# Moving four small packed matmul blocks of a batch: one adjacent pair in the slot, two singles behind the attention-score matmuls

## Chip, cores, metric

One core of one Trainium2 chip. The metric is the device time of one execution in microseconds (us). The experiments ran in three later calls, each with the kernel before beside it; the record names a different chip for each of these calls, so runs of different calls are best compared by their ratios to the kernel before.

## The reference, cut to what matters

```python
# q, k, v: (8, 8, 576, 64); p: (8, 8, 32, 64)
p_packed = sm_attn(p, k, v)             # 32 packed rows per head
out = sm_attn(q, p_packed, p_packed)    # second attention, over 32 rows only
x = out.transpose(0, 2, 1, 3).reshape(4608, 512)
h = x @ w_in                            # 512 -> 2048
y = (h * cos(h)) @ w_out                # 2048 -> 512
```

The kernel does not form `x`. Since `x` is attention weights times `p_packed`, it computes the product `p_packed @ w_in` ("PPW") once per batch, and then `h` as attention weights times PPW.

## The kernel before

It works batch by batch. A *slot* of a batch has 16 steps. Each has one *hidden block* (four matmuls of 288 columns, cosine on ScalarE, product on VectorE) and some *output matmuls* (512 columns, `fill`) of the batch before, which give TensorE other work while a product is pending. Between two slots stand the two kinds of attention scores. The four PPW blocks of the next batch (`ppw(b, 0..3)`) are placed in the slot, two steps apart.

All the matmuls below write to PSUM, the memory in which the pool `A` lies. A block can start only when a PSUM buffer is free, which is when the last instruction that reads it has ended.

```python
A = ctx.enter_context(tc.tile_pool(name="psA", bufs=3, space=PSUM))   # 3 buffers for ALL of these
def psa(dt=FP32):
    return A.tile([128, 2, 512 if dt == FP32 else 1024], dt, name="psA", tag="A")

def ppw(b, n):                      # L175: eight matmuls on 64x32 tiles of the array, side by side
    ...
    ps = psa()
    for x in range(4):
        for y in range(2):
            r = slice(64 * y, 64 * y + 64)
            nc.tensor.matmul(ps[32 * x:32 * x + 32, y, :], ppT[b % 2][r, 2 * x + y, :],
                             w_in_bf[r, x, n * 512:(n + 1) * 512], start=True, stop=True)
    copy((V, ACT)[n % 2], PPW[b][:, :, n * 512:(n + 1) * 512], ps)

def h_mm(b, fc):                    # one hidden block
    ps = psa()
    ...                             # 4 matmuls, 128x128
    ACT.activation(out=csv, in_=ps[:, :, 0:HS], func=AF.Sin, bias=pihalf)
    def rest():
        V.tensor_tensor(out=gT..., in0=ps[:, :, 0:HS], in1=csv, op=ALU.mult)   # frees ps
        ...
    return rest

def slot(s, pieces, hooks):
    left = filler[1]
    for fc in range(NFC):           # 16 steps
        rest = h_mm(s, fc)
        while pieces and pieces[0][0] == fc:
            pieces.pop(0)[1]()
        rest()
        while hooks and hooks[0][0] == fc:
            hooks.pop(0)[1]()
        done = left - filler[1]
        fill((left * (fc + 1)) // NFC - done)

for s in range(2, B):
    ...
    s2(s)                           # second-stage scores: 64x32 tiles, two psa() buffers
    fill(8)
    if nxt:
        s1(s + 1)                   # first-stage scores of the next batch: the same
        ...
    fill(4); sums2(s, 0); fill(5); sums2(s, 1); normalise(s); fill(13)
    pieces = [(1, pw(2, 2)), (4, pw(2, 3))] if s == 2 else []
    if nxt:
        pieces += [(5, lambda: pp(s + 1))] + [(8 + 2 * n, pw(s + 1, n)) for n in range(4)]
    slot(s, pieces, [])
```

Matmuls run in the order of the program, and `psa()` hands out the three buffers in the order in which their last readers stand in the program.

The softmax here doesn't subtract the row's maximum and nothing guards it: scores larger than these inputs give would overflow.

Of the kernel before, what the change touches and what calls it, by code (L numbers as in the profile page):

```python
# [15 lines left out]
def kernel(  # L16
# [37 lines left out]
    V, ACT, G = nc.vector, nc.scalar, nc.gpsimd  # L54

    w_in_bf = const.tile([128, 4, DF], BF16, name="w_in_bf")
    w_out_bf = const.tile([128, NFC, DM], BF16, name="w_out_bf")
# [5 lines left out]
    p_raw = const.tile([128, 2 * B, D], FP32, name="p_raw")  # L63
    p_bf = const.tile([128, 2 * B, 2, D], BF16, name="p_bf")
# [6 lines left out]
    a2u, lns, a2n, PPW = {}, {}, {}, {}  # L71

    def copy(eng, out, in_):
        if eng is ACT:
            ACT.copy(out=out, in_=in_)  # L75
        else:
            eng.tensor_copy(out=out, in_=in_)  # L77

    def psa(dt=FP32):
        return A.tile([128, 2, 512 if dt == FP32 else 1024], dt, name="psA", tag="A")  # L80

    def load(n, b):
        bf[n, b] = bf_pool.tile([TP, H, C * D], BF16, name=n + "bf", tag=n + "bf")
        G.dma_start(out=bf[n, b], in_=srcs[n][b].rearrange("h (p c) d -> p h (c d)", c=C))  # L84
# [6 lines left out]
    def xbar(n, b):  # L91
        t = xT[n, b] = att_pool.tile([128, H * 3, TP], BF16, name=n + "T", tag=n + "T")
        nc.sync.dma_start_transpose(out=t, in_=bf[n, b].rearrange("p h x -> p (h x)"))
# [13 lines left out]
    def pack_p(b0, b1):  # L107
        ng = 2 * (b1 - b0)
        ps = psa(BF16)
        flat = ps.rearrange("p a x -> p (a x)")  # L110
        for g in range(ng):
            nc.tensor.transpose(flat[:, g * 128:(g + 1) * 128],
                                p_bf[:, 2 * b0 + g].rearrange("p t d -> p (t d)"), ident)
        V.tensor_copy(out=P2[:, b0:b1].rearrange("p b h n -> p (b h n)"), in_=flat[:, 0:ng * 128])

    def scores(lhs, rhs):
        ps = []
        for y in range(2):
            t = psa()
            for x in range(4):  # L120
                for e in range(2):
                    r = slice(64 * e, 64 * e + 64)
                    h = 2 * x + y
                    nc.tensor.matmul(t[32 * x:32 * x + 32, e, 0:HS], lhs[r, h, :],  # L124
                                     rhs[r, 3 * h:3 * h + 3, :], start=True, stop=True)
            ps.append(t)
        return ps

    def s1(b):
        ps = scores(P2[:, b], xT["k", b])  # L130
        sm = small.tile([128, 2], FP32, name="sums1")
        for y in range(2):
            ACT.activation(  # L133
                out=a1[b % 2][:, y, :, 0:TP].rearrange("p (e m) x -> p e m x", e=2),
                in_=ps[y][:, :, 0:HS].rearrange("p e (m x) -> p e m x", m=3),
                func=AF.Exp, scale=scale, accum_out=sm[:, y:y + 1])
        sums1[b] = sm
# [20 lines left out]
    def pp(b):  # L158
        ps = psa()
        for hp in range(4):  # L160
            for j in range(C):
                c = 2 * (j % 3) + j // 3
                nc.tensor.matmul(ps[:, 0, hp * 64:(hp + 1) * 64], vp[b][:, c, hp * 128:(hp + 1) * 128],  # L163
                                 a1T[b][0:TP, :, j, 32 * hp:32 * hp + 32], start=(j == 0), stop=(j == C - 1))
        pv = ps[:, 0, 0:256].rearrange("p (a y x) -> p a y x", a=4, y=2)
        t = ppT[b % 2].rearrange("p (a y) x -> p a y x", y=2)
        for y in range(2):
            r = slice(64 * y, 64 * y + 64)
            V.tensor_copy(out=t[r, :, y, :], in_=pv[r, :, y, :])
        for y in range(2):  # L170
            r = slice(64 * y, 64 * y + 64)
            z = slice(64 - 64 * y, 128 - 64 * y)
            ACT.copy(out=t[z, :, y, :], in_=pv[r, :, y, :])  # L173

    def ppw(b, n):  # L175
        if b not in PPW:
            PPW[b] = ppw_pool.tile([128, 2, DF], BF16, name="PPW", tag="PPW")
        ps = psa()
        for x in range(4):
            for y in range(2):  # L180
                r = slice(64 * y, 64 * y + 64)
                nc.tensor.matmul(ps[32 * x:32 * x + 32, y, :], ppT[b % 2][r, 2 * x + y, :],  # L182
                                 w_in_bf[r, x, n * 512:(n + 1) * 512], start=True, stop=True)
        copy((V, ACT)[n % 2], PPW[b][:, :, n * 512:(n + 1) * 512], ps)

    def s2(b):
        a2u[b] = att_pool.tile([128, 2, S], BF16, name="a2u", tag="a2u")
        ps = scores(ppT[b % 2], xT["q", b])
        for y in range(2):
            ACT.activation(out=a2u[b][:, y].rearrange("p (e x) -> p e x", e=2),  # L190
                           in_=ps[y][:, :, 0:HS], func=AF.Exp, scale=rs1[b][:, y:y + 1])
# [91 lines left out]
    def set_filler(b):  # L283
        fill(1000)
        filler[0] = out_gen(b)
        filler[1] = 16 * n_chunks(b)

    def fill(n):
        while n > 0 and filler[1] > 0:
            next(filler[0])  # L290
            filler[1] -= 1
            n -= 1

    def load_w_in(n):
        G.dma_start(out=w_in_bf[:, :, n * 512:(n + 1) * 512],
                    in_=moe_w_in.rearrange("(a p) n -> p a n", p=128)[:, :, n * 512:(n + 1) * 512])

    def load_w_out(n):
        G.dma_start(out=w_out_bf[:, n * 4:(n + 1) * 4, :],
                    in_=moe_w_out.rearrange("(a p) n -> p a n", p=128)[:, n * 4:(n + 1) * 4, :])  # L300

    def dup_p(a, b):
        for t in range(2):
            V.tensor_copy(out=p_bf[:, a:b, t, :], in_=p_raw[:, a:b, :])

    def load_w_in(n):
        G.dma_start(out=w_in_bf[:, :, n * 512:(n + 1) * 512],
                    in_=moe_w_in.rearrange("(a p) n -> p a n", p=128)[:, :, n * 512:(n + 1) * 512])

    def load_w_out(n):  # L310
        G.dma_start(out=w_out_bf[:, n * 4:(n + 1) * 4, :],
                    in_=moe_w_out.rearrange("(a p) n -> p a n", p=128)[:, n * 4:(n + 1) * 4, :])

    def dup_p(a, b):
        for t in range(2):
            V.tensor_copy(out=p_bf[:, a:b, t, :], in_=p_raw[:, a:b, :])

    def warm(n):
        for _ in range(n):
            nc.tensor.matmul(wps, wz[:, 0:128], wz, start=True, stop=True)  # L320
# [41 lines left out]
    pe_T("q", 0, (V, ACT, V))  # L362
    s2(0)
    ppw(0, 0)
    sums2(0, 0)
    sums2(0, 1)
# [42 lines left out]
    def slot(s, pieces, hooks):  # L409
        left = filler[1]  # L410
        for fc in range(NFC):
# [9 lines that stand above are left out]
    def pw(b, n):  # L421
        return lambda: ppw(b, n)

    def begin_loads(b):
        G.tensor_copy(out=gate, in_=xT["k", b][0:1, 0, 0:1])
        for n, i in (("v", b), ("q", b), ("k", b + 1)):
            load(n, i)
# [2 lines left out]
    xbar("q", 2)  # L430
    xbar("k", 3)
    slot(1, [(1, pw(1, 2)), (4, pw(1, 3)), (7, lambda: pp(2)), (9, lambda: pack_p(3, B)),
             (11, pw(2, 0)), (14, pw(2, 1))], [(8, lambda: begin_loads(3))])

    for s in range(2, B):
        nxt = s + 1 < B
        set_filler(s - 1)
        ACT.preload_act_table_set(EXP_SET)  # L438
        if nxt:
            permute_v(s + 1)  # L440
        s2(s)
        fill(8)
        if nxt:
            s1(s + 1)
            xbar("q", s + 1)
            if s + 2 < B:
                xbar("k", s + 2)
            a1_xbar(s + 1)
            recips(s + 1)
            G.tensor_copy(out=gate, in_=a1T[s + 1][0:1, 0, 0, 0:1])  # L450
        fill(4)
        sums2(s, 0)
        fill(5)
        sums2(s, 1)
        normalise(s)
        fill(13)
        for n, b in (("v", s + 2), ("q", s + 2), ("k", s + 3)):
            if b < B:
                load(n, b)
        pieces = [(1, pw(2, 2)), (4, pw(2, 3))] if s == 2 else []  # L460
        if nxt:
            pieces += [(5, lambda: pp(s + 1))] + [(8 + 2 * n, pw(s + 1, n)) for n in range(4)]
        slot(s, pieces, [])
        fill(1000)
    set_filler(B - 1)
# [32 lines left out]
```

## Time and profile before

| | before |
|---|---|
| median | 264.84 us (264.78 to 265.21, 3 runs) |
| TensorE (PE) busy | 244.6 of 263.0 us |
| ScalarE (ACT), VectorE (DVE) busy | 182.7, 158.5 us |

From the page of the kernel before, its first part: busy time, share of the span, number of instructions for each engine.

```profile
PE 244.6 (93%) x2037; PEld 132.1 (50%) x2037; DVE 158.5 (60%) x248; ACT 182.7 (69%) x276; POOL 53.5 (20%) x67
```

TensorE is the limit. What counts is what it does that is not streaming of columns. The next lines are the PE part of the timeline of the kernel before, slot 4 (columns: start, duration, engine, line, operation, operands, number merged). L221 is a hidden block, L271 output matmuls, L182 a PPW block. `128*128` and `64*32` are the sizes of the tiles into which the array is divided: the tiling mode. A PPW block and the scores use 64x32 tiles, the other matmuls shown here the whole array.

```profile
153.59 0.65 PE L221 MATMUL psA<-a2n,PPW 128*128 128x288 bf16 x4
154.17 0.41 PE L182 MATMUL psA<-w_in_bf,ppT 64*32 64x512 bf16 x8
154.51 0.82 PE L271 MATMUL ot<-w_out_bf,gT 128*128 128x512 bf16 x3
155.17 0.65 PE L221 MATMUL psA<-a2n,PPW 128*128 128x288 bf16 x4
155.66 0.81 PE L271 MATMUL ot<-w_out_bf,joint 128*128 128x512 bf16 x3
156.31 0.65 PE L221 MATMUL psA<-a2n,PPW 128*128 128x288 bf16 x4
```

Read starts, not durations: matmuls overlap. The step from 155.17 to 156.31 has no PPW block and takes 1.14 us. The step from 153.59 to 155.17 has one and takes 1.58 us. So a block costs 0.44 us, and 512 columns stream in only about 0.215 us (three 512-column output matmuls, from 155.66 to 156.31, take 0.65). The other 0.23 us is on both sides of the block. The Trainium skill, "TensorEngine Tiling (Array Packing)", Key Properties, states that changing the tiling mode drains the TensorE; this trace agrees in that each change costs time, and it gives the size. Whether all of it is the drain, or a part is the weight loads at the boundary, is open; "mode change" below means the 0.23 us.

The end of slot 4 in the same kernel, with the lines of ScalarE and VectorE that matter. L225 is the cosine, L228 the product, L124 the scores (two kinds), L190 the exponential of the second-stage scores.

```profile
160.62 0.65 PE L221 MATMUL psA<-a2n,PPW 128*128 128x288 bf16 x4
161.31 0.74 ACT L225 ACTIVATE cosT<-psA,pihalf 128x576 bf16<-128x576 f32 x1
162.06 0.44 PE L124 MATMUL psA<-qT,ppT 64*32 64x288 bf16 x16
162.08 0.76 DVE L228 TENSOR_TENSOR gT<-psA,cosT 128x576 bf16<-128x576 f32 x1 [0.82 <-ACT cosT L225]
162.43 1.90 PE L271 MATMUL ot<-w_out_bf,gT 128*128 128x512 bf16 x8
164.26 0.32 PE L124 MATMUL psA<-kT,P 64*32 64x288 bf16 x8
164.86 0.32 PE L124 MATMUL psA<-kT,P 64*32 64x288 bf16 x8 [0.28 <-ACT a2u L190]
```

The last hidden block starts at 160.62, and its buffer is free at 162.84, when the product ends: 2.22 us. The scores pass without a wait, because they take older buffers. The first-stage scores at 164.26 wait half-way for an exponential (the bracket shows the idle time and its cause).

Four lines of the list of waits of PE in the kernel before (columns: total us, times, longest). The wait in the last line lies in the start-up, at 25 us, and is not of a slot:

```profile
PE psA L221 <- DVE gT L228: 3.1, 10, 0.5
PE psA L124 <- ACT a2u L190: 1.1, 3, 0.5
PE psA L221 <- DVE PPW L77: 0.7, 2, 0.5
PE psA L182 <- DVE gT L228: 0.6, 1, 0.6
```

### The profile page before, as it was taken

How to read it: one execution, taken by the hardware profiler on the slowest of the kernel's cores; microseconds unless marked ns; L12 is line 12 of the kernel's file. 1: busy time of each engine (PE TensorE's matmuls, PEld its weight loads, DVE VectorE, ACT ScalarE, POOL GpSimd, SP SyncE). 2: the span in 40 equal slices, each digit the busy share in tenths (PEclk: the TensorE clock that was granted, in tenths of full speed). 3: DMA queues.
4: the chain of work that ended last, by engine and by line, in shares of the span. 5: the costliest groups of instructions: out<-in, count | busy, mean ns of one | idle time of the engine just before them, and what ended most of it. 6: DMA issues, size and time to landing. Idle time of an engine off the chain costs nothing.

```text
span 263.0 us, 5065 instructions
## 1 busy us (share of the span) xinstructions
PE 244.6 (93%) x2037; PEld 132.1 (50%) x2037; DVE 158.5 (60%) x248; ACT 182.7 (69%) x276; POOL 53.5 (20%) x67
## 2 busy tenths in 40 slices
PE   8758779998989999999999999999999999999993
PEld 3433446455534555456445644464446554565452
DVE  2446886748853787358835685378735873578110
ACT  1358882497698757987798768877897678886000
POOL 8523002440422220504050302220040000000000
PEclk9997999999999999999999999999999999999998
DMA  6999999999399899399949992899194111111232
GB/s 95 203 226 206 206 204 197 192 186 201 47 203 203 189 165 187 73 193 173 221 95 184 168 221 75 159 188 176 47 158 113 40 42 40 40 46 36 80 82 80
DMA packets 62919, 37.09 MB, mean 141 GB/s; under 512 B 35520, under 2 KB 58304, under 8 KB 62896
## 3 DMA queue, kind: packets, MB, share of 16 engines
q0 software_dynamic: 23168, 18.81, 47.1%
q1 hardware_dynamic: 39568, 17.83, 31.5%
q8 instruction: 16, 0.26, 0.4%
q10 hardware_dynamic: 160, 0.13, 0.2%
q14 instruction: 7, 0.06, 0.1%
HBM read 37.22 MB, written 9.44 MB: 177 GB/s over the span
## 4 chain that ended last, share of the span: by engine, by line
PE 66%; DMA 13%; ACT 9%; DVE 7%; issue 2%; POOL 1%; DVEq 0%; ACTq 0%; POOLq 0%
PE ot L271 39%; PE psA L221 17%; DMA kbf<-in_k_dram 7%; DMA w_in_bf<-in_moe_w_in_dram 5%; DVE gT L228 4%; ACT cosT L225 3%; PE psA L182 2%; PE psA L163 2%; DVE PPW L77 2%; ACT PPW L75 1%; ACT L438 1%; PE psA L124 1%; PE ot L260 1%; PE psA L198 1%; PE psA L102 1%
## 5 line engine op out<-in xcount | busy, mean ns | idle before, releaser
L271 PE MATMUL ot<-w_out_bf,gT 128*128 128x512 bf16 x512 | 132.1, 380 | 0.0
L225 ACT ACTIVATE cosT<-psA,pihalf 128x576 bf16<-128x576 f32 x128 | 94.0, 742 | 32.0 <-PE psA L221 30.7
L228 DVE TENSOR_TENSOR gT<-psA,cosT 128x576 bf16<-128x576 f32 x128 | 94.9, 754 | 33.7 <-ACT cosT L225 32.6
L221 PE MATMUL psA<-a2n,PPW 128*128 128x288 bf16 x512 | 83.4, 285 | 5.5 <-DVE gT L228 3.1
L221 PEld LDWEIGHTS <-PPW 128*128 128x128 bf16 x512 | 49.9, 97 | 43.0 <-issue 13.0
L271 PEld LDWEIGHTS <-gT 128*128 128x128 bf16 x512 | 47.0, 98 | 42.8 <-issue 7.1
L232 POOL COPY joint<-gT 128x512 bf16<-128x512 bf16 x16 | 9.7, 614 | 111.1 <-DVE gT L228 111.1
L208 DVE SCALAR_TENSOR_TENSOR a2n<-a2u,r,lns 128x576 bf16<-128x576 bf16 x16 | 12.4, 815 | 20.1 <-ACT lns L206 20.1
L77 DVE COPY osb<-ot 128x512 f32<-128x512 f32 (+1 forms) x19 | 12.7, 670 | 15.1 <-PE ot L271 12.0
L75 ACT COPY osb<-ot 128x512 f32<-128x512 f32 (+1 forms) x18 | 10.3, 574 | 15.0 <-PE ot L271 10.1
L77 DVE CAST PPW<-psA 128x1024 bf16<-128x1024 f32 x16 | 19.5, 1220 | 1.5 <-PE psA L182 1.2
L75 ACT CAST PPW<-psA 128x1024 bf16<-128x1024 f32 x16 | 16.1, 1005 | 2.6 <-PE psA L182 2.6
L77 POOL COPY vp<-vbf 96x3072 bf16<-96x3072 bf16 x6 | 16.5, 2749 | 1.2 <-DMA vbf<-in_v_dram 1.2
L182 PE MATMUL psA<-w_in_bf,ppT 64*32 64x512 bf16 x256 | 13.4, 393 | 2.2 <-DMA w_in_bf<-in_moe_w_in_dram 1.5
L271 PE MATMUL ot<-w_out_bf,joint 128*128 128x512 bf16 x48 | 12.9, 380 | 0.0
L190 ACT ACTIVATE a2u<-psA,rs 128x576 bf16<-128x576 f32 x16 | 11.0, 738 | 2.5 <-PE psA L124 2.4
L200 ACT ACTIVATE lns<-psA 128x576 f32<-128x576 f32 x16 | 10.5, 658 | 2.3 <-PE psA L198 2.3
L133 ACT ACTIVATE a<-psA 128x576 bf16<-128x576 f32 x16 | 10.3, 651 | 2.6 <-PE psA L124 2.6
L173 ACT CAST ppT<-psA 64x128 bf16<-64x128 f32 x16 | 4.2, 260 | 10.8 <-PE psA L102 6.5
L142 DVE RECIPROCAL r<-sums 128x2 f32<-128x2 f32 x8 | 1.3, 160 | 16.5 <-ACT a L133 16.5
L84 POOL DMA_DIRECT2D kbf<-in_k_dram x8 | 6.3, 786 | 21.2 <-PE psA L102 17.3
L320 PE MATMUL wps<-wz 128*128 128x512 bf16 x25 | 9.4, 537 | 1.2 <-DVE wz L342 1.2
(55 smaller groups left out, 152.4 us busy)
## 6 DMA issues: line engine op xcount, KB each, us to landing
kbf<-in_k_dram POOLq DMA_DIRECT2D x8, 576.0 KB, 11.4
vbf<-in_v_dram POOLq DMA_DIRECT2D x8, 576.0 KB, 6.8
qbf<-in_q_dram POOLq DMA_DIRECT2D x8, 576.0 KB, 9.4
out_dram<-osb SPq DMA_DIRECT2D x24, 192.0 KB, 2.8
out_dram<-osb SPq DMA_DIRECT2D x22, 128.0 KB, 2.4
w_in_bf<-in_moe_w_in_dram POOLq DMA_DIRECT2D x4, 512.0 KB, 15.3
w_out_bf<-in_moe_w_out_dram POOLq DMA_DIRECT2D x4, 512.0 KB, 20.2
out_dram<-osb SPq DMA_DIRECT2D x26, 64.0 KB, 2.2
```

Source lines behind the costliest of these rows:

```text
L75: ACT.copy(out=out, in_=in_)
L77: eng.tensor_copy(out=out, in_=in_)
L133: ACT.activation(out=a1[b % 2][:, y, :, 0:TP].rearrange("p (e m) x -> p e m x", e=2), in_=ps[y][:, :, 0:HS].rearrange("p e (m x) -> p e m ...
L182: nc.tensor.matmul(ps[32 * x:32 * x + 32, y, :], ppT[b % 2][r, 2 * x + y, :], w_in_bf[r, x, n * 512:(n + 1) * 512], start=True, stop=True)
L190: ACT.activation(out=a2u[b][:, y].rearrange("p (e x) -> p e x", e=2), in_=ps[y][:, :, 0:HS], func=AF.Exp, scale=rs1[b][:, y:y + 1])
L200: ACT.activation(out=lns[b][:, y].rearrange("p (e x) -> p e x", e=2), in_=ps[:, :, 0:HS], func=AF.Ln)
L208: V.scalar_tensor_tensor(out=a2n[b][:, y], in0=a2u[b][:, y], scalar=r1[b][:, y:y + 1], in1=lns[b][:, y], op0=ALU.mult, op1=ALU.mult)
L221: nc.tensor.matmul(ps[:, e, 0:HS], PPW[b][:, y, fc * 128:(fc + 1) * 128], a2n[b][:, y, e * HS:(e + 1) * HS], start=(y == 0), stop=(y == 1))
L225: ACT.activation(out=csv, in_=ps[:, :, 0:HS], func=AF.Sin, bias=pihalf)
L228: V.tensor_tensor(out=gT[b][:, fc, :].rearrange("p (e x) -> p e x", e=2), in0=ps[:, :, 0:HS], in1=csv, op=ALU.mult)
L232: G.tensor_copy(out=joint[b // 2][:, fc - 7:fc + 1, j0:j0 + 64], in_=gT[b][:, fc - 7:fc + 1, 512:576])
L271: nc.tensor.matmul(ps, w, w_out_bf[:, fc, :], start=(fc == 0), stop=(fc == NFC - 1))
```

## The change

The intent is to pay for fewer mode changes. Blocks 0 and 1 of the next batch stand next to each other in the slot, with four output matmuls on each side; blocks 2 and 3 stand right behind score matmuls, which already use 64x32 tiles. The casts of blocks 2 and 3 both go to VectorE. (The diff also deletes function definitions that stood there twice; that changes no instruction.)

```diff
-    def ppw(b, n):
+    def ppw(b, n, eng=None):
...
-        copy((V, ACT)[n % 2], PPW[b][:, :, n * 512:(n + 1) * 512], ps)
+        copy(eng or (V, ACT)[n % 2], PPW[b][:, :, n * 512:(n + 1) * 512], ps)
...
+    def pw2(b):
+        fill(4)
+        ppw(b, 0)
+        ppw(b, 1)
+        fill(4)
...
-             (11, pw(2, 0)), (14, pw(2, 1))], [(8, lambda: begin_loads(3))])     # slot 1
+             (12, lambda: pw2(2))], [(8, lambda: begin_loads(3))])
...
         s2(s)
+        ppw(s, 2, V)
         fill(8)
         if nxt:
             s1(s + 1)
+            ppw(s, 3, V)
...
+        else:
+            ppw(s, 3, V)
...
-        pieces = [(1, pw(2, 2)), (4, pw(2, 3))] if s == 2 else []
-        if nxt:
-            pieces += [(5, lambda: pp(s + 1))] + [(8 + 2 * n, pw(s + 1, n)) for n in range(4)]
+        pieces = [(5, lambda: pp(s + 1)), (9, lambda: pw2(s + 1))] if nxt else []
```

More of the change, by code (lines that the diff above doesn't have):

```diff
@@ L292, in fill @@
             n -= 1
-    def load_w_in(n):
-        G.dma_start(out=w_in_bf[:, :, n * 512:(n + 1) * 512],
-                    in_=moe_w_in.rearrange("(a p) n -> p a n", p=128)[:, :, n * 512:(n + 1) * 512])
-    def load_w_out(n):
-        G.dma_start(out=w_out_bf[:, n * 4:(n + 1) * 4, :],
-                    in_=moe_w_out.rearrange("(a p) n -> p a n", p=128)[:, n * 4:(n + 1) * 4, :])
-    def dup_p(a, b):
-        for t in range(2):
-            V.tensor_copy(out=p_bf[:, a:b, t, :], in_=p_raw[:, a:b, :])
     def load_w_in(n):
```

## The prediction

> **What bounds the kernel now.** TensorE. The page's first part shows PE busy 244.6 of 263.0 us (93%), VectorE 60%, ScalarE 69%; the list of waits gives PE about 12 us in all, much of it in the warm-up. The granted clock is 0.99. In the slots (16 hidden blocks of a batch, output matmuls between) the timeline shows an undisturbed step of four 288-column and three 512-column matmuls taking 1.135 us, pure streaming (0.12 and 0.2135 us each).
>
> **What the change saves.** A packed-times-w_in block is eight 64x32-tile matmuls that stream together. A step with one takes 1.58 us in the timeline, so a block costs 0.445 us: about 0.21 streaming and 0.23 into and out of the tile mode. The Trainium skill, "TensorEngine Tiling (Array Packing)", Key Properties, says that changing the tiling mode drains the TensorE; the trace agrees (0.10 us before, 0.13 us after the block). Two adjacent blocks should cost 0.66 instead of 0.89 us; a block directly behind score matmuls, already in that mode, 0.21. Intended saving: 0.23 + 2 x 0.23 = 0.69 us a batch, six batches, less one block without scores before it: about 3.9 us (1.5%). The work is unchanged, except that one eviction a batch goes from ScalarE (1.00 us) to VectorE (1.22 us).
>
> **What it costs.** There are only three PSUM buffers of tag A, reused in order of release.
> 1. The second-stage scores take the buffers of hidden blocks 13 and 14; the block behind them needs that of block 15, free only when its cosine and product are done, 2.22 us after block 15 began (timeline: 160.62 to 162.84). PE is done with the scores at 1.45 to 1.7 us. It waits 0.6 to 0.8 us, in order. So this block costs 0.8 to 1.0 us, more than its 0.445 us before, in every batch.
> 2. The first-stage scores then reuse both second-stage score buffers, so wait for both exponentials, not one; but PE comes later: 0 to 0.3 us, against 0.5 us three times now.
> 3. The pair in the slot: the next hidden block takes the first pair buffer, whose VectorE cast ends about 1.65 us after the pair began; pair and four output matmuls cover 1.4 us. About 0.3 us of wait. In slots with only two output matmuls a step (odd ones) the eight used up around the pair leave three hidden blocks without any: another 0.85 us, waiting for products. These slots already lose 0.5 us so.
> From hidden block 8 to the end of the next scores: slot 1: +0.3, slot 2: -0.1, slot 3: +0.5, slot 4: 0 to +0.2, slot 5: +0.15, slot 6: +0.3 us. Sum about +1.1 us, all on the critical path, since PE is the chain.
>
> **Prediction.** The saving in mode changes is real but is paid back in new PSUM waits: 265.9 us, 263.0 to 268.3 (8 in 10). Chances: faster by over 2% 0.04, within 2% 0.91, slower by over 2% 0.05.
>
> **What would show it.** PE busy stays or falls by some 2 us, and PE's waits rise by 5 to 6 us: packed blocks waiting for the product (VectorE gT) six times, 0.5 to 0.8 us each; hidden blocks waiting for the PPW cast about 0.3 us, five or six times. The issue gap before packed blocks' weight loads falls from 7.7 us by about half. The second single, behind the first-stage scores, adds only 0.2 us.
>
> **What would make it wrong.** If PE's wait for block 15 is shorter (another buffer order), up to 4 us is gained. If VectorE, with three of four casts, delays products or normalising more than I count, 2 us worse.

## The result, and the profile after

265.53 us median (265.42 to 265.63, 4 runs), against 265.02 us (264.78 to 265.79, 4 runs) for the kernel before. The ratio is 1.0018, with a 95% interval of 0.9999 to 1.0038: no difference clear of the noise. (A ratio is the mean time of one kernel's fast runs over that of the other's of the same rounds, so it is not quite the ratio of the medians.)

The first part of the page after:

```profile
PE 239.9 (91%) x2004; PEld 133.6 (51%) x2037; DVE 166.3 (63%) x254; ACT 178.4 (68%) x270; POOL 53.5 (20%) x67
```

PE is less busy and the time is not shorter. Two warnings go with this line. There are 33 fewer matmul records than weight loads, so some are missing from this trace. And busy time counts overlapping, modelled durations: the Trainium skill, "Perfetto Trace Analysis", Identifying the Most-Contended Engine, says that matmul busy time is not a good measure of how close a kernel is to its roofline, because matmuls are pipelined. Busy time fell by 4.7 us while the span rose by 0.8. The missing records need not be the reason: e3 below has the same instructions and all 2037 records, and shows 240.6 us. The starts and the waits are what can be used.

The pair in slot 4 after the change, PE with the casts:

```profile
154.21 0.62 PE L182 MATMUL psA<-w_in_bf,ppT 64*32 64x512 bf16 x16
154.70 1.23 DVE L77 CAST PPW<-psA 128x1024 bf16<-128x1024 f32 x1 [0.84 <-PE psA L182]
154.77 0.60 PE L271 MATMUL ot<-w_out_bf,gT 128*128 128x512 bf16 x2
155.21 0.59 PE L271 MATMUL ot<-w_out_bf,joint 128*128 128x512 bf16 x2
155.97 1.14 PE L221 MATMUL psA<-a2n,PPW 128*128 128x288 bf16 x8 [0.17 <-DVE PPW L77]
```

From 154.21 to 154.77 the pair takes 0.56 us, plus 0.1 us to get in: 0.66 as predicted, instead of 0.89. But the next hidden block needs the pair's first buffer, whose cast ends at 155.93. Four output matmuls (0.215 us each) last from 154.77 to 155.64 only, so the block starts 0.33 us late. The bracket shows 0.17: the matmul before it is still counted as busy for the rest.

Slots 3 and 5 have only two output matmuls a step, and the eight around the pair leave three hidden blocks without any. PE in slot 5 after the change:

```profile
183.64 1.63 PE L221 MATMUL psA<-a2n,PPW 128*128 128x288 bf16 x12 [0.17 <-DVE PPW L77]
185.91 0.65 PE L221 MATMUL psA<-a2n,PPW 128*128 128x288 bf16 x4 [0.64 <-DVE gT L228]
```

The three blocks stream in 0.49 us each, to 185.11, so the next one starts 0.80 us late, waiting for a product. Slot 3 shows the same.

The end of slot 4 after the change:

```profile
160.65 0.65 PE L221 MATMUL psA<-a2n,PPW 128*128 128x288 bf16 x4
161.34 0.74 ACT L225 ACTIVATE cosT<-psA,pihalf 128x576 bf16<-128x576 f32 x1 [0.40 <-PE psA L221]
162.09 0.44 PE L124 MATMUL psA<-qT,ppT 64*32 64x288 bf16 x16
162.11 0.76 DVE L228 TENSOR_TENSOR gT<-psA,cosT 128x576 bf16<-128x576 f32 x1 [0.38 <-ACT cosT L225]
162.92 0.41 PE L182 MATMUL psA<-w_in_bf,ppT 64*32 64x512 bf16 x8 [0.39 <-DVE gT L228]
163.26 1.90 PE L271 MATMUL ot<-w_out_bf,gT 128*128 128x512 bf16 x7
165.09 0.44 PE L124 MATMUL psA<-kT,P 64*32 64x288 bf16 x16
165.52 0.41 PE L182 MATMUL psA<-w_in_bf,ppT 64*32 64x512 bf16 x8
165.86 0.39 PE L271 MATMUL ot<-w_out_bf,gT 128*128 128x512 bf16 x1
```

The block behind the second-stage scores starts at 162.92, 0.05 us after the product of the last hidden block ended (162.87), and everything behind it waits too. The Trainium skill, "TensorE: Matmul & The Clock Gate", Part 3, The mechanism, says that matmuls run in strict order; the trace agrees: the next output matmul, which does not need the block, starts only at 163.26. From the scores to the next output matmul there are now 1.17 us, against 0.37 before: this block costs 0.80 us, in a place where the intent was 0.21. The block behind the first-stage scores needs no fresh mode change.

The list of waits of PE after:

```profile
PE psA L221 <- DVE gT L228: 3.6, 9, 0.6
PE psA L182 <- DVE gT L228: 2.7, 6, 0.6
PE psA L221 <- DVE PPW L77: 2.1, 8, 0.6
PE psA L124 <- DVE gT L228: 1.0, 2, 0.6
```

PPW blocks wait for products six times, once in each changed batch. Hidden blocks wait for PPW casts eight times instead of two; the six new ones stand behind the six pairs. The wait of first-stage scores for exponentials (1.1 us) is gone.

By slot, in us, from the start of the second row-sum matmul group of one batch to that of the next, read from the timelines ("both mended" is an experiment below). The start-up ahead of the first of these marks ended between 53.9 and 54.5 us in the profiled executions, which is why slots are compared and not spans:

| slot | before | after | both mended |
|---|---|---|---|
| 1 | 27.06 | 28.11 | 26.91 |
| 2 | 30.20 | 29.25 | 28.58 |
| 3 | 26.30 | 26.95 | 25.83 |
| 4 | 29.54 | 29.53 | 28.86 |
| 5 | 27.27 | 26.92 | 26.27 |
| 6 | 28.64 | 29.02 | 28.13 |
| sum | 169.01 | 169.78 | 164.58 |

Slots 1 and 2 belong together: two blocks of batch 2, which stood in slot 2 before, now stand ahead of it.

### The profile page after: what moved, and what is told of

It is laid out like the page before. It is cut to its first block, busy times and chain, and to the rows that moved or that the text cites. A ratio compares the mean times of both kernels' runs of the same rounds, so it can differ in the third digit from the quotient of the medians.

```text
span 263.8 us, 5032 instructions
## 1 busy us (share of the span) xinstructions
PE 239.9 (91%) x2004; PEld 133.6 (51%) x2037; DVE 166.3 (63%) x254; ACT 178.4 (68%) x270; POOL 53.5 (20%) x67
## 4 chain that ended last, share of the span: by engine, by line
PE 70%; DMA 13%; DVE 8%; ACT 5%; issue 2%; POOL 1%; DVEq 0%; ACTq 0%; POOLq 0%
PE ot L271 40%; PE psA L221 20%; DMA kbf<-in_k_dram 7%; DMA w_in_bf<-in_moe_w_in_dram 5%; DVE gT L228 3%; DVE PPW L77 3%; PE psA L182 3%; ACT cosT L225 3%; PE psA L163 2%; PE ot L260 1%; PE psA L198 1%; PE psA L124 1%; PE psA L102 1%; ACT PPW L75 1%; DVE a2n L208 1%
## 5 line engine op out<-in xcount | busy, mean ns | idle before, releaser
L271 PE MATMUL ot<-w_out_bf,gT 128*128 128x512 bf16 x484 | 126.0, 379 | 1.9 <-issue 0.8
L225 ACT ACTIVATE cosT<-psA,pihalf 128x576 bf16<-128x576 f32 x128 | 92.8, 740 | 28.8 <-PE psA L221 27.7
L221 PEld LDWEIGHTS <-PPW 128*128 128x128 bf16 x512 | 50.6, 99 | 44.4 <-issue 15.4
L271 PEld LDWEIGHTS <-gT 128*128 128x128 bf16 x512 | 47.7, 98 | 43.2 <-issue 6.9
L77 DVE CAST PPW<-psA 128x1024 bf16<-128x1024 f32 x22 | 26.9, 1224 | 13.5 <-PE psA L182 13.5
L182 PE MATMUL psA<-w_in_bf,ppT 64*32 64x512 bf16 x256 | 12.1, 389 | 4.2 <-DVE gT L228 2.7
L75 ACT CAST PPW<-psA 128x1024 bf16<-128x1024 f32 x10 | 10.1, 1010 | 6.5 <-PE psA L182 6.5
L308 PE MATMUL wps<-wz 128*128 128x512 bf16 x23 | 8.8, 543 | 1.5 <-DVE wz L330 1.2
```

The source lines that it names most:

```text
L75: ACT.copy(out=out, in_=in_)
L77: eng.tensor_copy(out=out, in_=in_)
L221: nc.tensor.matmul(ps[:, e, 0:HS], PPW[b][:, y, fc * 128:(fc + 1) * 128], a2n[b][:, y, e * HS:(e + 1) * HS], start=(y == 0), stop=(y == 1))
L271: nc.tensor.matmul(ps, w, w_out_bf[:, fc, :], start=(fc == 0), stop=(fc == NFC - 1))
```

## The experiments

Theory: fewer mode changes do save 0.23 us each, and two new waits for PSUM buffers give it back (the product of the last hidden block; the pair's first cast), with the steps that the pair leaves without output matmuls. Rivals: adjacency saves nothing; the pair alone is to blame; VectorE, with three of the four casts, is the new limit; the two waits hide behind one another.

| run | median us | ratio to before (95%) |
|---|---|---|
| the change | 265.53 | 1.0018 (0.9999 to 1.0038) |
| e1 pair only | 268.25 | 1.0118 (1.0100 to 1.0137) |
| e2 singles only | 263.71 | 0.9950 (0.9935 to 0.9965) |
| e3 four outputs first, four after | 263.86 | 0.9957 (0.9942 to 0.9972) |
| e4 product before casts | 263.81 | 0.9959 (0.9936 to 0.9982) |
| e5 four outputs first, six after | 262.10 | 0.9888 (0.9868 to 0.9908) |
| e6 the four between scores and block | 263.30 | 0.9933 (0.9916 to 0.9950) |
| e7 e5 and e4 together | 260.08 | 0.9810 (0.9789 to 0.9830) |
| e8 e5 without the pair | 260.80 | 0.9840 (0.9820 to 0.9860) |
| e9 the kernel before with e5's move | 264.16 | 0.9972 (0.9954 to 0.9991) |
| e10 e7, no pair in slots 3 and 5 | 259.67 | 0.9803 (0.9786 to 0.9820) |
| e11 e7, pair parted by one output | 261.81 | 0.9882 (0.9865 to 0.9900) |

All gave correct results. The kernel before, run again (e1 to e4, e5 to e8, e9 to e11), had medians of 265.19, 264.98 and 264.74 us.

### e1: only the pair

```diff
         s2(s)
-        ppw(s, 2, V)
         fill(8)                      # and no ppw(s, 3, V) behind s1
...
+        pieces = [(1, pw(2, 2)), (4, pw(2, 3))] if s == 2 else []
-        pieces = [(5, ...pp), (9, ...pw2(s + 1))] if nxt else []
+        pieces += [(5, ...pp), (9, ...pw2(s + 1)), (12, pw(s + 1, 2)), (14, pw(s + 1, 3))]
```

> Only the pair half of the change; blocks 2 and 3 go back into the slot as singles (steps 12 and 14), ScalarE takes block 3 again. Theory (savings are real, PSUM waits pay them back): 0.23 us a batch saved by adjacency, about 0.2 to 0.5 us a batch lost to the wait for the pair's cast and to the steps without output matmuls: 264.5 to 265.5 us, PE waits hidden<-PPW cast near 2 us. Rival A (no wait matters, the pair just saves two mode changes a batch): 263.5 us. Rival B (the pair is what costs everything): at or above the change's 265.5 us.

Measured: 268.25 us, 1.2% slower than the kernel before. The theory and rival A had it far too fast; only rival B's "at or above 265.5" holds. The timeline of slot 4 shows what I had not counted:

```profile
157.59 0.38 PE L271 MATMUL ot<-w_out_bf,joint 128*128 128x512 bf16 x1
157.87 0.65 PE L221 MATMUL psA<-a2n,PPW 128*128 128x288 bf16 x4
158.07 1.42 DVE L228 TENSOR_TENSOR gT<-psA,cosT 128x576 bf16<-128x576 f32 x2 [0.25 <-ACT cosT L225]
158.88 0.41 PE L182 MATMUL psA<-w_in_bf,ppT 64*32 64x512 bf16 x8 [0.36 <-DVE gT L228]
```

The pair uses up eight output matmuls, so the steps behind it have few. Block 2 at step 12 meets buffers that are still being read, and waits for a product. The list of waits has 3.1 us of this, six times, against 0.6 us, once, before; five of the six are of this kind, in the slots, and the sixth is the one in the start-up. So this run does not price the pair as it stands in the change; it shows that the output matmuls around the pair are taken from steps that needed them. The pair inside the change is priced by e2.

### e2: only the singles

```diff
-             (12, lambda: pw2(2))], ...
+             (11, pw(2, 0)), (14, pw(2, 1))], ...
...
-        pieces = [(5, ...pp), (9, ...pw2(s + 1))] if nxt else []
+        pieces = [(5, ...pp), (8, pw(s + 1, 0)), (10, pw(s + 1, 1))] if nxt else []
```

> Only the singles half; blocks 0 and 1 of the next batch stay separate in the slot (steps 8 and 10), without extra output matmuls around them. Theory: the block behind the second-stage scores waits 0.4 to 0.6 us for the product of hidden block 15, six times (2.5 to 3 us in all), which cancels the mode changes saved: 264.5 to 265.5 us. Rival A (adjacency saves and nothing waits): 262.5 us. Rival B (the pair costs everything, singles save): about 262.5 us too, with the wait shown being harmless.

Measured: 263.71 us, 0.5% faster than before, and faster than I expected. The wait was there (PPW blocks for products, 3.8 us, seven times, of which 0.6 us in the start-up). I had left out two gains of the same move: the first-stage scores no longer wait for exponentials (1.1 us before, absent from this run's list), and slots 3 and 5, now with two blocks fewer, took 26.19 and 26.64 us against 26.30 and 27.27. So, as written, the pair makes the change 1.8 us slower than its singles alone, although it takes away a mode change. This bears on rival B: the singles, with their wait, are a net gain of 1.5 us, and the pair with its eight output matmuls is what turns it into a net loss. The two runs came out between the theory and rival B; that the singles' wait costs time as well is shown by e3 and e5.

### e3: four output matmuls ahead of the scores

```diff
+        fill(4)
         s2(s)
         ppw(s, 2, V)
-        fill(8)
+        fill(4)
```

> The change, but four of the eight output matmuls behind the first single go ahead of the second-stage scores; same instructions. Theory: the 0.85 us of work covers the wait for hidden block 15, so packed<-gT falls from 2.7 us to below 0.5 and scores<-gT from 1.0 to below 0.3; a new wait of the first-stage scores for the exponentials (0.1 to 0.4 us, six times at most) takes back a part: 262.8 to 264.2 us. Rival C (the time is lost to the load on VectorE, which has three of four casts, not to the order of the buffers): unchanged, 265.5 us.

Measured: 263.86 us. The same instructions on every engine, and 1.7 us less than the change. PE's waits:

```profile
PE psA L124 <- ACT a2u L190: 1.3, 5, 0.3
PE psA L182 <- DVE gT L228: 1.0, 2, 0.6
```

The wait for products fell from 2.7 to 1.0 us. Of this, 0.64 us is the wait in the start-up, which the change's trace happens to lack; at the new place only 0.35 us is left, in batch 2, within the expected 0.5. The expected new wait for exponentials appeared, 1.3 us. VectorE's load is unchanged, so it is not what had cost these 1.7 us.

### e4: the product before the pair's casts

```diff
-        pieces = [(5, ...pp), (9, lambda: pw2(s + 1))] if nxt else []
-        slot(s, pieces, [])
+        pieces = [(5, ...pp)] if nxt else []
+        hooks = [(9, lambda: pw2(s + 1))] if nxt else []      # hooks run behind rest()
+        slot(s, pieces, hooks)                                # slot 1: the same, at step 12
```

> The change, but the product of the step's hidden block is issued before the pair, so that the next hidden block takes that buffer rather than the pair's first one. Same instructions. Theory: hidden<-PPW cast falls from 2.1 us to below 1; hidden<-gT falls a little in odd slots; about 0.2 to 0.3 us a batch: 264.0 to 264.8 us. Rival (the cast wait is only where other waits show up): waits move to hidden<-gT and the time stays at 265.5 us.

Measured: 263.81 us, a little better than the expected range. In slot 4 the next hidden block starts as soon as the output matmuls are through:

```profile
153.50 0.62 PE L182 MATMUL psA<-w_in_bf,ppT 64*32 64x512 bf16 x16
153.52 0.76 DVE L228 TENSOR_TENSOR gT<-psA,cosT 128x576 bf16<-128x576 f32 x1 [0.38 <-ACT cosT L225]
154.19 1.21 DVE L77 CAST PPW<-psA 128x1024 bf16<-128x1024 f32 x1
154.93 1.18 PE L221 MATMUL psA<-a2n,PPW 128*128 128x288 bf16 x8
```

It starts 1.43 us after the pair, against 1.76 in the change: the 0.33 us is gone. It now takes the buffer of its own step's hidden block, free at 154.28, and not the one whose cast ends at 155.40. Hidden blocks' waits for PPW casts fell from 2.1 to 1.1 us.

### e5 and e6: with adjacency and without, both without most of the wait

```diff
+        fill(4)                # e5: here           e6: not here
         s2(s)
+        # e6: fill(4) here
         ppw(s, 2, V)
-        fill(8)
+        fill(6)                # both
...
-        fill(4); sums2(s, 0); fill(5); ...
+        fill(3); sums2(s, 0); fill(4); ...     # both
```

> Four output matmuls ahead of the second-stage scores and six behind the block (three and four instead of four and five later; the total is the change's own). Theory: the wait of the first-stage scores for the exponentials, which took back a part in the version with four and four (1.3 us), falls below 0.5; packed<-gT stays below 1.2: 263.0 to 263.7 us.

> As the version with four first and six behind, but the four go between the second-stage scores and the block: the same instructions and buffers, no wait for hidden block 15 either, only the block is no longer adjacent to scores, so there is one more mode change in and out in each of six batches. Theory (a change in and out costs 0.23 us): 0.8 to 1.4 us slower than its neighbour in this call (a part may be hidden where the first-stage scores wait). Rival (adjacency to the scores is worth nothing, only the waits matter): the same time within 0.3 us.

Measured: e5 262.10 us, better than expected; its wait for exponentials is 0.5 us, twice. e6 263.30 us, 1.2 us slower than e5, in the expected 0.8 to 1.4. The PE timelines of e5, first, and e6 at the same place:

```profile
160.51 0.44 PE L124 MATMUL psA<-qT,ppT 64*32 64x288 bf16 x16
160.76 0.40 PE L182 MATMUL psA<-w_in_bf,ppT 64*32 64x512 bf16 x8
162.50 0.32 PE L124 MATMUL psA<-kT,P 64*32 64x288 bf16 x8
163.08 0.32 PE L124 MATMUL psA<-kT,P 64*32 64x288 bf16 x8 [0.27 <-ACT a2u L190]
```

```profile
161.07 0.44 PE L124 MATMUL psA<-qT,ppT 64*32 64x288 bf16 x16
161.45 1.04 PE L271 MATMUL ot<-w_out_bf,gT 128*128 128x512 bf16 x4
162.41 0.41 PE L182 MATMUL psA<-w_in_bf,ppT 64*32 64x512 bf16 x8
164.16 0.67 PE L124 MATMUL psA<-kT,P 64*32 64x288 bf16 x16
```

In e5 the block starts 0.25 us behind the scores, which is their streaming alone. In e6 the scores take 0.38 us to the next matmul, and the block starts 0.96 us after the first of four output matmuls, which stream in 0.86 us. But at this place e5 gives the gain back: its first-stage scores wait half-way for an exponential, and those of e6, which come later, do not. By slot, e6 is slower than e5 by 0.55, 0.23, 0.24, 0.00, 0.00 and 0.23 us (slots 1 to 6). In slots 2, 3 and 6 the two have the same waits, and the mode change is worth the predicted 0.23 us; in slots 4 and 5 the exponentials hide it; in slot 1 both kernels still wait for products (its last three hidden blocks have no output matmul between them), so its 0.55 us is not the mode change alone. Adjacency to the scores pays, once nothing waits there.

### e7: both mended

The edits of e5 and e4 together.

> Four outputs first, six behind, and the product issued before the pair's casts. Theory: the two waits are separate, so the two gains add: 261.5 to 262.3 us, below the kernel before by 1 to 1.3%. Rival (they share one slack): no better than 263.3 us.

Measured: 260.08 us, 1.9% faster than the kernel before. Relative to the change, e5 gave 3.4 us, e4 1.7 us, and both 5.5 us: the gains add, at the least, so the two waits are separate. I had expected 261.5 to 262.3, because I had e5 too small.

### e8 and e10: is the pair worth it now?

e8 is e5 with blocks 0 and 1 single (the edit of e2). e10 is e7 with that edit only in the slots with two output matmuls a step:

```diff
+        if nxt and s % 2:
+            pieces += [(8, pw(s + 1, 0)), (10, pw(s + 1, 1))]
-        hooks = [(9, lambda: pw2(s + 1))] if nxt else []
+        hooks = [(9, lambda: pw2(s + 1))] if nxt and s % 2 == 0 else []
```

> The two singles with four outputs first and six behind, and no pair: blocks 0 and 1 stay separate in the slot. Theory: without the pair's waits and without its saving: 262.0 to 262.6 us, within 0.5 us of the version with both waits mended, a little slower in slots 2, 4 and 6 (0.2 us each, the mode change) and a little faster in slots 3 and 5.

> Both waits mended, the pair kept only in slots 1, 2, 4 and 6, where the steps have enough output matmuls or did well; in slots 3 and 5 blocks 0 and 1 are single at steps 8 and 10. From the intervals of the versions with and without the pair: slot 3 saves 0.4 us, slot 5 about nothing: 259.6 to 260.0 us.

Measured: e8 260.80, better than expected (I again had the move of output matmuls too small), and 0.7 us slower than e7. So the mended pair gains where the unmended one lost (e5, with it, is 1.3 us slower than e8). By slot, e8 is slower than e7 in slots 1, 4 and 6 (27.48, 29.06, 28.33 us), equal in 2 and 5 (within 0.03), and faster in slot 3 (25.39 against 25.83): slots 2 to 6 together come out even, and slot 1 makes the difference. e10 took 259.67 us, inside the expected range: slot 3 took 25.38 us and the others, but for slot 2, are within 0.03 us of e7's. Slot 2, where e10 changes nothing, took 28.38 us against 28.58: so much can differ between two executions. e10 is 2.0% below the kernel before. That it beats e7 is not shown: by the ratios it is 0.2 us, and the intervals overlap.

### e9: the control

The kernel before, with e5's move of output matmuls and nothing else.

> Control: the kernel before the change, with the same move of output matmuls (four ahead of the second-stage scores, six behind, three and four later) and nothing else. If the move helps by itself, it is by taking away the first-stage scores' wait for the exponentials (1.1 us shown, three times): 263.3 to 264.3 us. Rival (the gain of the mended version is the move, not the adjacent blocks): 262 us or below.

Measured: 264.16 us, 0.3% faster than before, as expected. The move alone gives 0.7 us by the ratio; the rest of e7's 5 us needs the change. The first-stage scores' wait for exponentials is gone from its list. Its profiled execution also shows one wait of 1.0 us for the transposed load of the softmax weights in slot 5, which the profile of the kernel before lacks; whether the earlier scores cause it is not settled.

### e11: the pair parted

```diff
         ppw(b, 0)
+        fill(1)
         ppw(b, 1)
-        fill(4)
+        fill(3)
```

> Both waits mended, but one of the four output matmuls behind the pair goes between its two blocks: one more mode change in and out in each of six slots, same instructions and nearly the same casts. Theory: 0.23 us in slots 2, 4 and 6, and up to that in 1, 3 and 5, where a wait for the product may hide a part: 0.7 to 1.4 us slower than the version with both waits mended (260.1), so 260.8 to 261.5 us. Rival (adjacency of the pair saves nothing): 260.1 us.

Measured: 261.81 us, 1.7 us more than e7 (by the ratios 0.9882 and 0.9810, 1.9 us). The direction and the rival's fall are clear; the size is above my range. By slot it loses 0.44, 0.13, 0.23, 0.19, 0.23 and 0.33 us (slots 1 to 6, 1.54 us together). Slots 3, 4 and 5 fit one mode change. Slots 1 and 6 lose more and slot 2 less; why, I did not look into. The expected difference between odd and even slots is not there.

## Why the prediction was right

The prediction was 265.9 us, within 263.0 to 268.3; measured were 265.53 us. Point by point:

- *A block costs 0.445 us, of which 0.23 is the mode change; a pair costs 0.66.* Right: 0.66 us in slot 4, and e6 against e5 prices the change of mode at 0.23 us in the three slots where the two have the same waits.
- *The block behind the second-stage scores waits for the product of block 15 and costs 0.8 to 1.0 us.* Right: 0.80 us in slot 4; in slot 3 the same reading gives 1.38 - 0.37 = 1.01 us. Batch 2, ahead of slot 2, is outside: 1.67 - 0.37 = 1.30 us, because there the scores themselves waited for products too. Six waits, as said. e3 and e5 show by removal that this wait and its neighbours held 1.7 to 3.4 us.
- *The second single adds 0.2 us.* Right: in slot 2 from first-stage scores to output matmul 0.59 us (108.80 to 109.39), against 0.37 before.
- *First-stage scores wait 0 to 0.3 us, not 0.5 us three times.* Right: the 1.1 us are gone from the list; in slot 4 the block behind them starts 0.43 us after them instead of 0.25, so at most 0.2 us is left.
- *The pair's cast makes the next hidden block about 0.3 us late.* Right: 0.33 us, and e4 removes it.
- *In odd slots three hidden blocks without output matmuls cost another 0.85 us.* Right: 0.80 us in slots 3 and 5. e4 does not remove this: in e4 and in e7 a hidden block still waits for a product in slots 3 and 5 (0.41 and 0.64 us shown).
- *By slot.* Slots 1 and 2 together +0.2 predicted, +0.10 measured; slot 3 +0.5 and +0.65; slot 4 0 to +0.2 and -0.01; slot 6 +0.3 and +0.38. Slot 5 was mis-sized: +0.15 predicted, -0.35 measured. I had taken it that its blocks cause the same waits before the change as those of slot 3; but from the first softmax-times-v matmul to the next scores, slot 3 shortened by 0.5 us and slot 5 by 0.87 us.
- *PE's waits rise by 5 to 6 us.* Too high: the list rises by some 3.3 to 4.4 us (depending on gaps of missing records), in part because it shows only a part of a delay (0.17 of 0.33 us).
- *The issue gap before PPW weight loads falls from 7.7 us by half.* Wrong: 30 gaps became 19, but their sum rose to 8.7 us. A weight load held back by the waiting block is put down to "issue" as well (0.60 us at 162.92), so this figure does not measure mode changes alone.

The slots sum to +0.77 us where about +1.1 was predicted, and most of the difference is slot 5. The range itself proves little, since it also holds the time of the kernel before; what speaks for the prediction is that the waits came where it said, in number and size. My expectations for the experiments were worse: e1, e2, e4, e5, e7, e8 and e11 fell outside the theory's range.

The experiments add what the prediction did not ask: the loss was not inherent. With both waits mended (e7) the kernel is 4.9 us faster than before, and 4.3 us faster, by the ratios, than the control e9. That is as much as the intended 3.9 us, but it is not shown to be the mode changes alone, since other waits moved too.

## What to carry to other kernels

Placing small-tile matmuls next to one another saves a mode change each time (0.23 us here), but the place must be chosen by which buffer the block will get: name the last reader of that buffer, and put enough independent matmuls ahead of the block to cover it. Where buffers go round in order of release, swapping two lines on another engine (the product before the cast) can move a wait away at no cost. And judge such a move in a stream of matmuls by start-to-start times and by ablation: busy time fell while the kernel was no faster, and two halves tested apart (+3.1 and -1.5 us) did not add up to the whole (+0.5).

## What the Trainium skill lacked or had wrong

- "TensorEngine Tiling (Array Packing)", Key Properties, says that a mode change drains the TensorE but gives no size: in this stream 0.10 us going in and 0.13 us coming out, 0.23 us for both, on top of 0.215 us of streaming.
- "Perfetto Trace Analysis" calls the end of a matmul an estimate, but does not say what follows for reading gaps: an idle time shown for PE understates how late a matmul starts by what the one before it is still counted as busy: 0.17 us were shown where the start was 0.33 us late.
